# The last tiles of a fused FFT and mixture-of-experts kernel: smaller routing batches, more scatters per tile, and an earlier step table

## The chip, the cores and the metric

One Trainium2 chip, one core of it. The metric is device time in microseconds (us) from launch to the end of the program, the median of several runs. The profile is one execution taken by the hardware profiler.

## What is computed

The reference runs three stages on `x` of shape (8, 3072, 256), all in float32:

```python
X = np.fft.fft(np.fft.fft(x, axis=1), axis=2).real          # 24576 tokens of 256
h = np.maximum(np.maximum(X @ w1, X @ w2), X @ w3)          # 768 hidden
x = h @ w_out                                               # 256
# second stage of experts, E = 8, top-1
skip = x @ w_skip                  # only tokens with skip > 0 are computed
e = argmax(x @ w_gate);  gate_w = softmax(x @ w_gate)[e]
out = x;  out[skip > 0] += gate_w * (relu(x @ W1[e]) @ W2[e])   # W1: 256x1024, W2: 1024x256
```

## The kernel before

The program has three parts, one after the other.

The first part computes the Fourier transform along the sequence and prepares the weights.

The second part (`moe_phase`) goes over 25 tiles of the transformed tokens: 0 to 22 have 8 blocks of 128 tokens, tile 23 has 4 blocks, tile 24 has 5. In period t (`period(t)`, twelve steps n = 0 to 11) the engines compute the hidden layer of tile t and the output layer of tile t-1. A step takes matmuls `pa`, `pb` (L483 to L485), VectorE combinations (L499 to L513), and a split of the result `ht` into a high and a low part, on ScalarE (L519) and GpSimd (L520). The output layer is `rest` (L555, result `zt` by L557), to which a linear term `lin` is added: `linear` makes two matmul groups, ScalarE copies each from PSUM (L546), GpSimd adds and subtracts them (L547, L549). The order on each engine is the order in which the code is written (`manual_schedule`): an instruction that waits holds all that stand behind it on its engine.

Beside this runs the routing, for a batch of tiles at a time (`BATCHES`): their gate scores come in a tile `st`; `finish` (L574 to L608, ten VectorE operations and one exponential on ScalarE) picks the expert and counts the tokens, `place` (L610 to L630, matmuls `pr` and four VectorE operations) computes each token's position in a list per expert, and `scatter` (L633) sends one block's 128 positions to that list in memory, by an indirect DMA on GpSimd. `fill()` does one VectorE step of the routing, and a step n of a period posts at most one scatter per half of `ht`. Before the batch that begins with tile 18 (`EARLY`), `choose` (15 more VectorE operations) picks one expert from the counts so far, for which three steps of 256 tokens are computed at fixed places (`STATIC` = 3).

Between the second part and the third stands the tail, from L1021 on. It finishes tile 24, posts the scatters that are left (each behind `apart()`, a small GpSimd addition on `idle`, L1002), and computes the static steps: `wide1` (48 matmuls L767), `wide1_rest` (VectorE, L771), `layer2_of` (24 matmuls L780 for each of two blocks), `result` (L784) and `place_rows` (L787). `table()` (L818) turns the counts into the table `tab` of all further steps: some 20 small VectorE operations, two transposes on TensorE and a copy. With `tab` SyncE loads the step's list entries `ida`, `idn`, `idm` and weights `ws`, and GpSimd gathers the rows `Gd` (L1110).

The third part is a loop over those steps (L1220, and a second one for half steps): `wide1`, transposes, `layer2_of`, each step with its own weights.

Buffers of the tail that matter here: `st` and `rI` (the positions) have 2 buffers each, `Gd` takes one of the two buffers in which the rows `Gs` of the second and third static step lie, and `acc`, `pz`, `pys` are PSUM.

Of the kernel before, what the change touches and what calls it, by code (L numbers as in the profile page):

```python
# [16 lines left out]
P = 128  # L17
# [15 lines left out]
STATIC = 3  # L33
BATCHES = [(3 * k, 3 * k + 1, 3 * k + 2) for k in range(7)] + [(21, 22), (23,), (24,)]
EARLY = 18
# [11 lines left out]
NK = 2  # L47
F1, F2, F3 = 3, 5, 6
TF = 23
T0 = 2  # L50
ENG = {mybir.EngineType.PE, mybir.EngineType.DVE, mybir.EngineType.Activation, mybir.EngineType.Pool}
# [357 lines left out]
def moe_phase(tc, a, sc, wt, wv, wp, gs, ident, out, lst, cpool):  # L409
    nc = tc.nc  # L410
    tiles = [(j, 0, 512, 0) for j in range(NT - 1)] + [(NT - 1, 0, 256, 0), (NT - 1, 256, 264, NB)]
    with (
# [122 lines left out]
        def layer2(t, hs, y, yk, zt):  # L535
            lin = {}

            def linear(c):
                lin[c] = mo.tile([P, 3, SW], F32, tag="ws", name="lin", bufs=2)
                for k in range(2):  # L540
                    pl = mq.tile([P, 512], F32, tag="pz", name="pl")
                    for n, (g, v) in enumerate(((0, 0), (0, 1), (1, 0))):
                        nc.tensor.matmul(pl[:, :SW], y[:, 2 * k + g, c * P : c * P + P], cc[:, k, v], start=n == 0, stop=k == 1 and n == 2)
                    if k == 0:
                        nc.tensor.matmul(pl[:, :SW], yk[:, c * P : c * P + P], wq, start=False, stop=True)
                    nc.scalar.activation(lin[c][:, k], pl[:, :SW], AF.Copy)  # L546
                nc.gpsimd.tensor_tensor(lin[c][:, 2], lin[c][:, 0], lin[c][:, 1], ALU.add)  # L547
                if (1, c) in bs:
                    nc.gpsimd.tensor_tensor(lin[c][:, 0], lin[c][:, 0], lin[c][:, 1], ALU.subtract)  # L549

# [59 lines left out]
        def place(first, nb, slots, _):  # L610
# [15 lines left out]
            yield  # L626
            ix = mr.tile([P, KB], I32, tag="rI", name="rI")[:, :nb]
            V.tensor_copy(ix, pos)
# [82 lines left out]
        moved = []  # L711
        zz = mr.tile([P, 2, 2], I32, name="zz", bufs=1)
        G, ids = [], []

# [182 lines left out]

        stage = {}

        def arrive(t, zt):  # L900
            k = next(k for k, ts in enumerate(BATCHES) if t in ts)
            if t == BATCHES[k][0]:
                stage["st"], stage["o"] = mr.tile([P, KB, 10], F32, tag="st", name="st"), 0
                nc.gpsimd.memset(stage["st"][:, :, E1:], 1e-9)
            ship(t, zt, stage["st"], stage["o"])
            stage["o"] += NBT[t]
            if t == BATCHES[k][-1]:
                waiting.append((k, stage["st"]))

        def period(t):  # L910
# [10 lines left out]
            for n in range(2 * NC6):  # L921
# [39 lines left out]
                for _ in range(HALF.get(n, 1)):  # L961
                    if half:
                        half.pop(0)()
                        if posted and (n < 9 or t + 1 < len(tiles)):
                            posted.pop(0)()
                if t == 0 and i == 1:
# [31 lines left out]

        idle = mr.tile([P, 2], I32, name="idle", bufs=1)

        def apart():
            nc.gpsimd.tensor_tensor(idle, zz[:, 0], zz[:, 0], ALU.add)  # L1002

        def post(n):
# [11 lines left out]

        nc.gpsimd.memset(zz, 0)
        cum = [mr.tile([P, 32], F32, name=f"cum{k}", bufs=1) for k in range(3)]
        for c in cum:
            nc.gpsimd.memset(c, 0.0)  # L1020
        with tc.manual_schedule(engines=ENG):  # L1021
# [47 lines left out]
            steps = table()  # L1069
            next(steps)  # L1070
            layer2_of(1, h, w, py[1])
            for k in range(1, STATIC):
                for b in range(2):
                    result(G[k - 1][:, b], py[b], ids[k - 1][:, b, 1:2].bitcast(F32), G[k - 1][:, b])
                    apart()
                    place_rows(ids[k - 1], b, G[k - 1][:, b])
                h = [hset() for _ in range(2)]
                ph = [acc("pb"), acc("pb"), acc("pb"), acc("pa")]
                for q in range(4):
                    wide1(x, w, h, q, ph[q])  # L1080
                    wide1_rest(h, q, ph[q])
                    if k == 1 and q == 2:
                        next(steps)
# [9 lines left out]
            idm, idn, ida, idc, idx = (mr.tile([P, 2, 2], I32, name=nm, bufs=1) for nm in ("idm", "idn", "ida", "idc", "idx"))  # L1093
            idb = ids[-1]
            dm = mr.tile([P, 4], F32, name="dm", bufs=1)
            gt = mr.tile([P, 2], I32, name="gt", bufs=1)
            W = [tuple(mh.tile([P, 1024], F32R, tag="ht", name="wd") for _ in range(2)) for _ in range(4)]
            ws = [mb.tile([P, 1024], F32, tag="u", name="ws", bufs=4) for _ in range(4)]
            w1s, w2s = ws[:2], ws[2:]
            Gd = mx.tile([P, 2, D], F32, tag="yb", name="Gd", bufs=2)  # L1100
            Z, Zn, O = (mz.tile([P, 2, D], F32, tag="zt", name=nm) for nm in ("Z", "Zn", "O"))
            load_ids(ida, 0)
            e1 = expert(0)
            load_w(w1s, "e1", e1)
            load_ids(idn, 1)
            load_ids(idm, 2)
            load_w(w2s, "e2", e1)

            def gather(idx, m):
# [3 lines left out]
                return r  # L1113
# [17 lines left out]
            fence_g()  # L1131
            ga += gather(idn, 2)
            for b in range(2):
# [3 lines left out]
        pys = [pys[2], mq.tile([P, 512], F32, tag="pz", name="pyd")]  # L1137
        for q in ga:
            for old in moved:
                tc.declare_no_dep(q.ins, old.ins, reason=why)  # L1140
        moved.extend(ga)
        nb = nc.values_load(nst[0:1, 0:1], min_val=0, max_val=P - 20)
# [254 lines left out]
```

## Time and profile before

| | |
|---|---|
| median of 3 runs | 1756.37 us (1752.12 to 1758.89) |
| the profiled execution | 1751.53 us, of which the span from first to last instruction is 1749.6 us |
| mean granted TensorE clock | 0.976 of full speed |
| busy: TensorE, VectorE, GpSimd, ScalarE | 93%, 77%, 64%, 42% of the span |

Full speed is 2.4 GHz, a granted clock of 0.5 is 1.2 GHz. In the rows, PE is TensorE, PEld its weight load, DVE VectorE, ACT ScalarE, POOL GpSimd, SP SyncE. What stands in brackets at the end of a row is how long the engine was idle before it, and what ended that.

### The profile page before, as it was taken

Reading aid. Unit: us, or ns where it says so; the run is one execution under the profiler, and the core shown is the slowest. Engines: PE = TensorE matmul, PEld = TensorE weight load, DVE = VectorE, ACT = ScalarE, POOL = GpSimd, SP = SyncE. Lnnn points to the kernel's source line nnn. Section 1 sums busy time; section 2 is a strip of 40 time slices with the busy share of each in tenths; the row PEclk is TensorE's granted clock in tenths of the full one; section 3 lists DMA queues with packets and bytes.
Section 4 is the critical chain, followed back from the end, with each engine's and each line's share of the span. In section 5 each row is a group of like instructions: output and inputs, shape, how many; then the busy total and the mean of one; then the engine's idle time right before and its main releaser. Section 6 shows DMA issues by size and latency. Waiting matters only on the chain. (4 is left out here: it accounts for less than half of the span.)

```text
span 1749.6 us, 33308 instructions
## 1 busy us (share of the span) xinstructions
PE 1628.1 (93%) x10837; PEld 1446.3 (83%) x10837; DVE 1347.5 (77%) x2288; ACT 734.7 (42%) x1437; POOL 1115.1 (64%) x1358
## 2 busy tenths in 40 slices
PE   6999699999999999999999999986689999999976
PEld 3665488888888888888888888886589999999976
DVE  8999488887887888888887878864367777777754
ACT  4545433333333333323333333322156666666654
POOL 2000356668769779779688687588646676766663
PEclk9999899999999999999999999989799999999989
DMA  8875411312111111111122111113256666666766
GB/s 327 309 264 204 140 61 43 121 40 58 43 43 44 43 43 43 55 43 43 55 44 50 54 43 40 40 30 90 59 184 219 217 228 225 222 224 226 226 196 218
DMA packets 109434, 212.47 MB, mean 121 GB/s; under 512 B 28107, under 2 KB 61292, under 8 KB 106228
## 3 DMA queue, kind: packets, MB, share of 16 engines
q1 hardware_dynamic: 94360, 188.65, 34.3%
q0 software_dynamic: 14112, 21.77, 4.0%
q8 instruction: 56, 0.92, 0.3%
q14 instruction: 42, 0.34, 0.2%
q10 hardware_dynamic: 864, 0.79, 0.1%
HBM read 157.82 MB, written 55.17 MB: 122 GB/s over the span
## 5 line engine op out<-in xcount | busy, mean ns | idle before, releaser
L520 POOL TENSOR_TENSOR ht<-u,ht 128x512 fp32r<-128x512 f32 (+2 forms) x300 | 374.1, 1252 | 184.2 <-ACT ht L519 181.4
L555 PE MATMUL pz<-wo,ht 128*128 128x266 f32 x3474 | 457.9, 287 | 0.6 <-DVE zt L557 0.6
L555 PEld LDWEIGHTS pz<-wo,ht 128*128 128x128 f32 x3474 | 444.8, 189 | 8.2 <-DVE zt L557 0.8
L519 ACT ACTIVATE ht<-u 128x512 fp32r<-128x512 f32 (+2 forms) x300 | 175.9, 610 | 534.4 <-DVE u L513 468.0
L633 POOL DMA_INDIRECT lst<-pair,rI x193 | 190.3, 986 | 35.6 <-issue 28.2
L767 PE MATMUL acc<-xd,wd 128*128 128x256 f32 x1632 | 193.4, 278 | 0.9 <-DVEq L1220 0.9
L767 PEld LDWEIGHTS acc<-xd,wd 128*128 128x128 f32 x1632 | 190.1, 188 | 1.1 <-issue 1.1
L811 DVE TENSOR_TENSOR wd<-ws,wd 128x1024 fp32r<-128x1024 f32 x150 | 177.5, 1225 | 16.5 <-issue 6.6
L810 ACT ACTIVATE wd<-ws 128x1024 fp32r<-128x1024 f32 x150 | 154.9, 1060 | 69.7 <-issue 43.7
L483 PE MATMUL pa<-y,wt 128*128 128x512 f32 (+2 forms) x300 | 126.1, 420 | 40.2 <-DVE u L499 27.4
L557 DVE TENSOR_TENSOR zt<-pz,lin 128x266 f32<-128x266 f32 x193 | 81.6, 432 | 88.5 <-PE pz L555 47.7
L780 PE MATMUL pys<-wd,hs 128*128 128x256 f32 x960 | 126.8, 288 | 0.5 <-DVE hs L771 0.5
L502 DVE TENSOR_TENSOR u<-u,pb 128x512 f32<-128x512 f32 (+2 forms) x150 | 99.2, 661 | 29.2 <-PE pb L485 28.4
L780 PEld LDWEIGHTS pys<-wd,hs 128*128 128x128 f32 x960 | 119.2, 192 | 1.4 <-DVE hs L771 0.9
L771 DVE SCALAR_TENSOR_TENSOR hs<-acc,hs 128x512 fp32r<-128x512 f32 x148 | 97.8, 687 | 29.2 <-ACT hs L768 25.8
L768 ACT ACTIVATE hs<-acc 128x512 fp32r<-128x512 f32 x148 | 86.3, 596 | 77.1 <-PE acc L767 71.8
L483 PE MATMUL pb<-y,wt 128*128 128x512 f32 (+2 forms) x300 | 118.1, 394 | 0.0
L484 PE MATMUL pb<-y,wt 128*128 128x512 f32 (+2 forms) x300 | 117.5, 392 | 0.0
L483 PEld LDWEIGHTS pa<-y,wt 128*128 128x128 f32 x300 | 57.4, 191 | 72.4 <-DVE u L499 59.5
L485 PE MATMUL pb<-y,wt 128*128 128x512 f32 (+2 forms) x300 | 117.2, 391 | 0.0
L485 PE MATMUL pa<-y,wt 128*128 128x512 f32 (+2 forms) x300 | 117.2, 391 | 0.0
L484 PE MATMUL pa<-y,wt 128*128 128x512 f32 (+2 forms) x300 | 117.0, 390 | 0.0
(286 smaller groups left out, 3205.2 us busy)
## 6 DMA issues: line engine op xcount, KB each, us to landing
ws<-e SPq DMA_DIRECT2D x164, 512.0 KB
xt<-xf SPq DMA_DIRECT2D x24, 1024.0 KB
out<-zt SPq DMA_DIRECT2D x48, 512.0 KB
yr<-ysc SPq DMA_DIRECT2D x25, 512.0 KB
ysc<-ytc SPq DMA_DIRECT2D x8, 768.0 KB
yb<-yfsc SPq DMA_DIRECT2D x23, 256.0 KB
ysc<-yts SPq DMA_DIRECT2D x8, 672.0 KB
wr<-wm SPq DMA_DIRECT2D x6, 768.0 KB
```

What stands on the lines that cost most here:

```text
L483: nc.tensor.matmul(pt[:, :w], wt[f][:, g, 0, c], hi, start=True, stop=False)
L484: nc.tensor.matmul(pt[:, :w], wt[f][:, g, 0, c], lo, start=False, stop=False)
L485: nc.tensor.matmul(pt[:, :w], wt[f][:, g, 1, c], hi, start=False, stop=not whole)
L502: nc.vector.tensor_tensor(minus_to, r, pb[:, :w], ALU.subtract)
L519: nc.scalar.activation(ht[:, 0, :w], h[:, s, :w], AF.Copy)
L520: nc.gpsimd.tensor_tensor(ht[:, 1, :w], h[:, s, :w], bits(ht[:, 0, :w]), ALU.subtract)
L555: nc.tensor.matmul(pz[:, :SW], hs[s][f][:, g, c * P : c * P + P], wo[:, v, f], start=f == 0 and g == 0 and v == 0, stop=f == NC6 - 1 and g ...
L633: ins = nc.gpsimd.indirect_dma_start(out=lst[:, :], out_offset=bass.IndirectOffsetOnAxis(ap=ix[:, b : b + 1], axis=0), in_=pair[:, first + b],
L767: nc.tensor.matmul(ph[:, f % 2 * 256 : f % 2 * 256 + 256], lhs, rhs, start=n == 0, stop=n == 5)
L780: nc.tensor.matmul(py[:, :D], lhs, rhs, start=n == 0, stop=n == 23)
L810: nc.scalar.activation(hi, r, AF.Copy)
L811: nc.vector.tensor_tensor(lo, r, bits(hi), ALU.subtract)
```

## The change

It has four edits, all for the end of the second part and the tail.

1. Batches: tiles 18 and 19 are one batch, 20 to 24 one each. Before, 18 to 20 were one, 21 and 22 one, 23 and 24 one each.
2. `rI` gets 4 buffers; the two `st` tiles are made once, with their padding set at the start of the program; from tile 20 on, every third step n posts two scatters with `apart()` between them.
3. For tiles from 21 on, ScalarE no longer copies the second half of the linear term; VectorE reads it from PSUM and does the addition and the subtraction.
4. In the tail: routing of tile 24 and the table's VectorE work come between the first and the second half of the first static step; the table's second part comes after the first half of its output layer; loads and the first gather of the loop's rows are issued within the static steps; `Gd` has a buffer of its own.

```diff
-BATCHES = [(3 * k, 3 * k + 1, 3 * k + 2) for k in range(7)] + [(21, 22), (23,), (24,)]
+BATCHES = [(3 * k, 3 * k + 1, 3 * k + 2) for k in range(6)] + [(18, 19)] + [(t,) for t in range(20, 25)]
-F1, F2, F3 = 3, 5, 6
+F1, F2, F4 = 3, 5, (4, 7)
+TL = 21
+TP = 20
...
-                    nc.scalar.activation(lin[c][:, k], pl[:, :SW], AF.Copy)
-                nc.gpsimd.tensor_tensor(lin[c][:, 2], lin[c][:, 0], lin[c][:, 1], ALU.add)
+                    if k == 0 or t < TL:
+                        nc.scalar.activation(lin[c][:, k], pl[:, :SW], AF.Copy)
+                eng, odd = (nc.gpsimd, lin[c][:, 1]) if t < TL else (nc.vector, pl[:, :SW])
+                eng.tensor_tensor(lin[c][:, 2], lin[c][:, 0], odd, ALU.add)
                 if (1, c) in bs:
-                    nc.gpsimd.tensor_tensor(lin[c][:, 0], lin[c][:, 0], lin[c][:, 1], ALU.subtract)
+                    eng.tensor_tensor(lin[c][:, 0], lin[c][:, 0], odd, ALU.subtract)
...
-            ix = mr.tile([P, KB], I32, tag="rI", name="rI")[:, :nb]
+            ix = mr.tile([P, KB], I32, tag="rI", name="rI", bufs=4)[:, :nb]
...
-        stage = {}
+        stage = {"n": 0, "sts": [mr.tile([P, KB, 10], F32, name=f"st{k}", bufs=1) for k in range(2)]}
+        for x in stage["sts"]:
+            nc.gpsimd.memset(x[:, :, E1:], 1e-9)
...
-                stage["st"], stage["o"] = mr.tile([P, KB, 10], F32, tag="st", name="st"), 0
-                nc.gpsimd.memset(stage["st"][:, :, E1:], 1e-9)
+                stage["st"], stage["o"] = stage["sts"][k % 2], 0
...
-                        if posted and (n < 9 or t + 1 < len(tiles)):
-                            posted.pop(0)()
+                        for k in range(2 if t >= TP and n % 3 == 0 else 1):
+                            if posted and (n < 9 or t + 1 < len(tiles)):
+                                if k:
+                                    apart()
+                                posted.pop(0)()
...
-            for _ in range(2):
-                fill()
-            for q in range(4):
+            for q in range(2):
+                for _ in range(F4[q]):
+                    fill()
                 wide1(x, w, h, q, ph[q])
-            for q in range(4):
-                for _ in range(F3):
-                    fill()
+            wide1_rest(h, 0, ph[0])
+            settle()
+            wide1_rest(h, 1, ph[1])
+            steps = table()
+            next(steps)
+            for q in range(2, 4):
+                wide1(x, w, h, q, ph[q])
+            for q in range(2, 4):
                 wide1_rest(h, q, ph[q])
-            settle()
...
             layer2_of(0, h, w, py[0])
+            next(steps)
...
+            Gd = mb.tile([P, 2, D], F32, tag="r", name="Gd", bufs=1)
+            e1 = expert(0)
+            load_w(w1s, "e1", e1)
+            load_ids(ida, 0)
+            load_ids(idn, 1)
+            load_ids(idm, 2)
+            load_w(w2s, "e2", e1)
...
             for k in range(1, STATIC):
+                if k + 1 == STATIC:
+                    apart()
+                    known(gather(ida, 2))
...
-            Gd = mx.tile([P, 2, D], F32, tag="yb", name="Gd", bufs=2)
...
-            apart()
-            ga = gather(ida, 2)
```

Where instructions stand, at the three places of which the prediction speaks. First TensorE in the first static step, from the end of the position matmuls `pr` of tile 24 on; before:

```order
L618 MATMUL pr<-sl,ones 128x9
L780 MATMUL pys<-wx,hs 128x256 x24
L750 MATMUL acc<-ident,Gs 128x128 x4
L823 LDWEIGHTS ones
L823 MATMUL pc<-sl,ones 128x8
L780 MATMUL pys<-wx,hs 128x256 x24
L767 MATMUL acc<-xs,wx 128x256 x36
L857 MATMUL pt<-ident,r_12993 1x128 x2
```

and now, where `pr` itself stands behind 24 of the step's 48 `acc` matmuls, not behind all:

```order
L622 MATMUL pr<-sl,ones 128x9
L833 LDWEIGHTS ones
L833 MATMUL pc<-sl,ones 128x8
L777 MATMUL acc<-xs,wx 128x256 x24
L790 MATMUL pys<-wx,hs 128x256 x24
L867 MATMUL pt<-ident,r_12947 1x128 x2
L760 MATMUL acc<-ident,Gs 128x128 x4
L790 MATMUL pys<-wx,hs 128x256 x24
```

The count `pc` for the table has moved ahead of the second half of the first step's `acc` matmuls, and the table's transposes `pt` have moved from within the second step to the middle of the first.

Second GpSimd at the end of the tail's scatters (`lst`); before:

```order
L633 DMA lst<-pair,rI 228480x2
L1002 TENSOR_TENSOR idle<-zz 128x2
L787 DMA out<-Gs,ids_11691 27776x256
L1002 TENSOR_TENSOR idle<-zz 128x2
L787 DMA out<-Gs,ids_11691 27776x256
L1002 TENSOR_TENSOR idle<-zz 128x2
L787 DMA out<-Gs,ids_11702 27776x256
L1002 TENSOR_TENSOR idle<-zz 128x2
L787 DMA out<-Gs,ids_11702 27776x256
L1002 TENSOR_TENSOR idle<-zz 128x2
L1110 DMA Gd<-out,ida 128x256 x2
```

and now:

```order
L637 DMA lst<-pair,rI 228480x2
L721 TENSOR_TENSOR idle<-zz 128x2
L797 DMA out<-Gs,ids_11253 27776x256
L721 TENSOR_TENSOR idle<-zz 128x2
L797 DMA out<-Gs,ids_11253 27776x256
L721 TENSOR_TENSOR idle<-zz 128x2
L1097 DMA Gd<-out,ida 128x256 x2
L721 TENSOR_TENSOR idle<-zz 128x2
L797 DMA out<-Gs,ids_11264 27776x256
```

The gather of the loop's first rows stands ahead of the second step's row scatters. Behind the last static gather (`Gs`), 34 of these list scatters stood in the tail before, now 15.

Third VectorE at the second output block of tile 23, in period 24; before:

```order
L583 TENSOR_TENSOR rd<-st,rm 128x16x8
L502 TENSOR_TENSOR pa<-r,pb 128x264
L587 SCALAR_TENSOR_TENSOR rd<-rd,kk 128x16x8
L557 TENSOR_TENSOR zt<-pz,lin 128x266
L590 TENSOR_REDUCE rv<-rd 128x16
```

and now:

```order
L587 TENSOR_TENSOR rd<-st_1373,rm 128x8x8
L504 TENSOR_TENSOR pa<-r,pb 128x264
L591 SCALAR_TENSOR_TENSOR rd<-rd,kk 128x8x8
L551 TENSOR_TENSOR lin<-lin,pl 128x266
L553 TENSOR_TENSOR lin<-lin,pl 128x266
L561 TENSOR_TENSOR zt<-pz,lin 128x266
L594 TENSOR_REDUCE rv<-rd 128x8
```

The two operations on `lin` are new on VectorE, directly ahead of the `zt` that needs them, and the routing operations beside them work on 8 blocks, not 16.

## Rows read from the trace of the kernel before

**Rows 1.** Busy time by stretch: periods 21 to 24, tail, static steps.

```profile
core 0: us, PE busy (x) PEld busy (x) DVE busy (x) ACT busy (x) POOL busy (x), PEclk, DMA share, GB/s
1042.55:1082.40 39.85, 38.99 (x246) 34.66 (x245) 31.86 (x55) 13.05 (x27) 35.84 (x35) 1.00 0.16 47
1082.40:1127.00 44.60, 41.19 (x251) 36.55 (x250) 38.99 (x80) 12.55 (x28) 23.24 (x24) 0.96 0.13 40
1127.00:1160.40 33.40, 32.34 (x273) 31.68 (x272) 21.85 (x60) 10.22 (x29) 25.18 (x33) 1.00 0.11 33
1160.40:1187.65 27.25, 21.05 (x144) 19.73 (x143) 19.46 (x59) 6.96 (x22) 21.62 (x26) 0.81 0.23 54
1187.65:1207.42 19.77, 19.13 (x159) 18.86 (x157) 10.40 (x29) 8.73 (x19) 15.02 (x20) 1.00 0.49 127
1207.42:1251.06 43.64, 15.10 (x110) 14.47 (x108) 10.08 (x31) 3.11 (x8) 35.06 (x61) 0.65 0.10 16
1251.06:1280.65 29.59, 25.04 (x204) 24.39 (x203) 14.34 (x34) 8.29 (x13) 11.75 (x19) 0.94 0.34 103
```

**Rows 2.** Timeline of TensorE, tail: start, duration, instruction, idle before it.

```profile
1207.42 5.81 PE L767 MATMUL acc<-xs,wx 128*128 128x256 f32 x48
...
1224.90 0.20 PE L616 MATMUL pr<-sl,tri 128*128 128x45 bf16 x1 [11.67 <-DVE sl L597]
...
1244.30 3.54 PE L780 MATMUL pys<-wx,hs 128*128 128x256 f32 x16 [16.86 <-DVE rS L604]
...
1251.06 4.26 PE L767 MATMUL acc<-xs,wx 128*128 128x256 f32 x36
...
1262.75 5.62 PE L767 MATMUL acc<-xs,wx 128*128 128x256 f32 x48
1268.21 2.88 PE L780 MATMUL pys<-wx,hs 128*128 128x256 f32 x24
1274.00 0.41 PE L750 MATMUL acc<-ident,Gd 128*128 128x128 f32 x2 [2.91 <-DMA Gd<-out,ida]
...
1275.52 4.25 PE L780 MATMUL pys<-wx,hs 128*128 128x256 f32 x24
```

**Rows 3.** Timeline of VectorE, tail.

```profile
1218.34 0.17 DVE L628 CAST rI<-rs 128x4 int32<-128x4 f32 x1 [14.28 <-DMA lst<-pair,rI]
...
1243.26 0.20 DVE L604 TENSOR_REDUCE rS<-st 128x5 f32<-128x45 f32 x1 [17.52 <-POOL st L904]
...
1249.56 0.16 DVE L825 TENSOR_TENSOR tf<-pc,kt 128x8 f32<-128x8 f32 x1
...
1253.54 0.15 DVE L853 TENSOR_SCALAR r<-r 128x1 f32<-128x1 f32 x1
```

**Rows 4.** Timeline of GpSimd, tail.

```profile
1202.32 1.00 POOL L633 DMA_INDIRECT lst<-pair,rI  x1 [0.17 <-issue]
...
1243.07 0.16 POOL L904 MEMSET st<- 128x24 f32 x1
...
1270.70 1.36 POOL L1110 DMA_INDIRECT Gd<-out,ida  x1 [5.76 <-issue]
```

**Rows 5.** Costliest groups of the page: busy, mean ns of one, idle before.

```profile
L771 DVE SCALAR_TENSOR_TENSOR hs<-acc,hs 128x512 fp32r<-128x512 f32 x148 | 97.8, 687 | 29.2 <-ACT hs L768 25.8
```

**Rows 6.** Timeline of TensorE, its longest waits in periods 22 and 24.

```profile
1113.25 0.51 PE L483 MATMUL pa<-y,wt 128*128 128x512 f32 x1 [3.12 <-DVE u L499]
...
1169.91 0.59 PE L483 MATMUL pa<-y,wt 128*128 128x264 f32 x1 [3.70 <-DVE u L499]
```

**Rows 7.** Timeline of VectorE, periods 22 and 24.

```profile
1097.05 0.98 DVE L690 TENSOR_TENSOR rc<-rc,ru 128x8 f32<-128x8 f32 x1
...
1168.83 0.43 DVE L557 TENSOR_TENSOR zt<-pz,lin 128x266 f32<-128x266 f32 x1 [4.38 <-POOL lin L547]
```

**Rows 8.** Timeline of GpSimd, beside the two rows of VectorE.

```profile
1096.71 1.30 POOL L520 TENSOR_TENSOR ht<-u,ht 128x512 fp32r<-128x512 f32 x1
...
1168.13 0.67 POOL L547 TENSOR_TENSOR lin<-lin 128x266 f32<-128x266 f32 x1
```

More of the change, by code (lines that the diff above doesn't have):

```diff
@@ L712, in moe_phase, with apart @@
         zz = mr.tile([P, 2, 2], I32, name="zz", bufs=1)
+        nc.gpsimd.memset(zz, 0)
+        idle = mr.tile([P, 2], I32, name="idle", bufs=1)
+        def apart():
+            nc.gpsimd.tensor_tensor(idle, zz[:, 0], zz[:, 0], ALU.add)
         G, ids = [], []
@@ L997, in moe_phase @@
         w = []
-        idle = mr.tile([P, 2], I32, name="idle", bufs=1)
-        def apart():
-            nc.gpsimd.tensor_tensor(idle, zz[:, 0], zz[:, 0], ALU.add)
         def post(n):
@@ L1015, in settle @@
             post(len(posted))
-        nc.gpsimd.memset(zz, 0)
         cum = [mr.tile([P, 32], F32, name=f"cum{k}", bufs=1) for k in range(3)]
@@ L1068, in moe_phase, with gather, known @@
             split_x(x, px)
-            steps = table()
-            next(steps)
             layer2_of(1, h, w, py[1])
+            idm, idn, ida, idc, idx = (mr.tile([P, 2, 2], I32, name=nm, bufs=1) for nm in ("idm", "idn", "ida", "idc", "idx"))
+            idb = ids[-1]
+            W = [tuple(mh.tile([P, 1024], F32R, tag="ht", name="wd") for _ in range(2)) for _ in range(4)]
+            ws = [mb.tile([P, 1024], F32, tag="u", name="ws", bufs=4) for _ in range(4)]
+            w1s, w2s = ws[:2], ws[2:]
+            Gd = mb.tile([P, 2, D], F32, tag="r", name="Gd", bufs=1)
[5 more added lines that the diff above has]
+            load_w(w2s, "e2", e1)
+            def gather(idx, m):
+                r = [nc.gpsimd.indirect_dma_start(
+                    out=Gd[:, b], out_offset=None, in_=out[:, :],
+                    in_offset=bass.IndirectOffsetOnAxis(ap=idx[:, b, 0:1], axis=0)) for b in range(m)]
+                return r
+            def known(ga):
+                for q in ga:
+                    for old in moved:
+                        tc.declare_no_dep(q.ins, old.ins, reason=why)
+                moved.extend(ga)
             for k in range(1, STATIC):
+                if k + 1 == STATIC:
+                    apart()
+                    known(gather(ida, 2))
                 for b in range(2):
@@ L1081, in moe_phase @@
                     wide1_rest(h, q, ph[q])
-                    if k == 1 and q == 2:
-                        next(steps)
                 if k + 1 == STATIC:
@@ L1092, in moe_phase @@
                 layer2_of(1, h, w, py[1])
-            idm, idn, ida, idc, idx = (mr.tile([P, 2, 2], I32, name=nm, bufs=1) for nm in ("idm", "idn", "ida", "idc", "idx"))
-            idb = ids[-1]
             dm = mr.tile([P, 4], F32, name="dm", bufs=1)
             gt = mr.tile([P, 2], I32, name="gt", bufs=1)
-            W = [tuple(mh.tile([P, 1024], F32R, tag="ht", name="wd") for _ in range(2)) for _ in range(4)]
-            ws = [mb.tile([P, 1024], F32, tag="u", name="ws", bufs=4) for _ in range(4)]
-            w1s, w2s = ws[:2], ws[2:]
-            Gd = mx.tile([P, 2, D], F32, tag="yb", name="Gd", bufs=2)
             Z, Zn, O = (mz.tile([P, 2, D], F32, tag="zt", name=nm) for nm in ("Z", "Zn", "O"))
[L1102 to L1109, printed above, removed]
-                r = [nc.gpsimd.indirect_dma_start(
-                    out=Gd[:, b], out_offset=None, in_=out[:, :],
-                    in_offset=bass.IndirectOffsetOnAxis(ap=idx[:, b, 0:1], axis=0)) for b in range(m)]
-                return r
             def fence_g():
@@ L1131, in moe_phase @@
             fence_g()
-            ga += gather(idn, 2)
+            known(gather(idn, 2))
             for b in range(2):
@@ L1137, in moe_phase @@
         pys = [pys[2], mq.tile([P, 512], F32, tag="pz", name="pyd")]
[L1138 to L1141, printed above, removed]
         nb = nc.values_load(nst[0:1, 0:1], min_val=0, max_val=P - 20)
```

## Prediction

> **What bounds the kernel now.** I read the busy shares over the whole span first, then cut the stretch around the change by its stages, then followed each engine's timeline through it. In the periods TensorE is the bound: 38.99 us of 39.85 in period 21. Then three stretches fall off [rows 1]. Period 22 takes 44.60 us instead of some 39.9; period 24 takes 27.25 with only 21.05 busy, at a granted clock of 0.81; and from the start of the static steps at 1207.42 to the loop at 1280.65, 73.2 us, TensorE is busy 40.1.
>
> The timeline of TensorE shows the tail's holes: 11.67 us ahead of the position matmuls of tile 24, 16.86 within the first output layer, 2.91 ahead of the loop's first rows [rows 2]. Each is followed to its cause on the engine that it waits for. The first: VectorE stood 14.28 us at the cast of the positions of tile 23, since that took a buffer from which scatters were still being read [rows 3]. The second: VectorE stood 17.52 us for the padding of `st`, a 0.16 us instruction on GpSimd that stood behind the scatters [rows 3, 4]. So both are the one queue of scatters. From 1202.32 to 1243.07 GpSimd posts 29 of them and one addition of 0.67: 1.38 us each [rows 4, 8]. The third hole is the gather, held 5.76 us on GpSimd [rows 4]. Its list entries come from a table that ended at 1253.69 [rows 3], and its buffer is that of a step whose rows were still being sent; I take the latter for the holder, since the rest of that wait fits nothing else.
>
> **The change part by part: the tail.** Without waits a static step takes 1262.75 - 1251.06 = 11.69 us [rows 2]; three are 35.1. What comes on top now:
> - The matmuls of positions and count: 0.3 us (`pr` 0.20 for its first, overlapped) [rows 2].
> - The wait for the routing of tile 24. It now stands behind half of `wide1`, 5.81 / 2 = 2.9 us. A small operation on VectorE costs some 0.19 (the table's 22 take 1253.54 + 0.15 - 1249.56 = 4.1) [rows 2, 3]. Eight of them lie ahead of the position matmuls, with one exponential and its two handovers: 1.5 to 3 us. Wait 0 to 2, I take 0.3.
> - The wait for the table. Between those matmuls and the last two `wide1_rest` VectorE has 6 small operations (1.1), two `wide1_rest` (0.69 each), the table (4.1) and then the third rest (0.69): 7.3 us [rows 3, 5]. TensorE meanwhile has the other half of `wide1` (2.9) and half an output layer (2.88 / 2): 4.3 [rows 2]. Wait 3.0.
> - The clock. After the wait of 2.91 the next 24 matmuls took 4.25 instead of 2.88 [rows 2]: I take 1.4. In period 24 the mean clock of 0.81 means 38% of 27.25 us, 10 us, at 1.2 GHz [rows 1], which is worth up to 5 us: that is the upper bound, and 0 the lower.
> - Entry of the loop: 0.9, the end of 4.25 behind 1275.52 to 1280.65 [rows 1, 2].
>
> Sum 35.1 + 0.3 + 0.3 + 3.0 + 1.4 + 0.9 = 41.0, against 73.2: **32.2 us less** (28 to 37).
>
> What covers the rest: 15 scatters are left in the tail, not 34, 20.7 us at 1.38. Begun at 1202.32 at the latest, they are out by 1223 [rows 4]. From the table's end to the arrival of the first rows it took 1274.00 - 1253.69 = 20.3 us before, the 5.76 included [rows 2 to 4]. The table now ends at 1207.4 + 2.9 + 0.6 + 6.6 = 1217.5; plus 20.3 is 1238; TensorE comes to those rows after 2.5 steps, at 1242. Four us of cover; beyond it each us late is a us lost. The weights `ws` start with the same table and have the same cover.
>
> **The periods.** Edit 3 takes 0.67 per operation off GpSimd, and puts one on VectorE that reads PSUM and SBUF as `zt` does, 0.43 [rows 7, 8]. Eight per full tile, four for tile 23: 5.4 and 2.7 us off GpSimd, 3.4 and 1.7 on VectorE. The added scatters: 16 each in periods 22 and 23, at 1.0 plus 0.17 [rows 4].
> - Period 24. VectorE waited 4.38 us for that addition on GpSimd, which stood among scatters, then TensorE 3.70 for VectorE, and then the clock fell [rows 1, 6, 7]. With the addition on VectorE this chain is gone. What bounds then is VectorE: 19.46 + 1.7, less half of the routing of 16 blocks (1): 20.2, and some 2 us in which it waits for the first output block. I take 22.5: **4.7 less** (1 to 7).
> - Period 22 lost 4.7 us to `choose` and to the routing of 24 blocks, which made VectorE late (38.99 busy, TensorE's longest wait 3.12) [rows 1, 6]. Now it has the routing of 8 blocks, the placing of 16, and 3.4 us of additions. VectorE's base is 31.9 (period 21) [rows 1]; with 3.4 and some 30 small operations (0.1 to 0.2 each, 4) it has 39, still near its limit: **2.6 less** (4.7 less to 1 more).
> - Period 21 gets `choose` and the routing of 16 blocks, so part of those 4.7: **3 more** (0 to 5).
> - Period 23: TensorE 32.34 of 33.40; VectorE 21.85 has room for 3.4 [rows 1]: **0** (1 less to 2 more).
>
> Edit 2's `rI` and `st` cost nothing in time: the padding's two instructions move to the program's start.
>
> Of the routing's operations one row is odd: 0.98 us for 128x8, where such a thing costs 0.16. It ends with a GpSimd addition that began 0.34 before it and ran 1.30 [rows 3, 7, 8]. So an operation with two inputs in SBUF stood until GpSimd was through. The Trainium skill has this as a rule (SBUF — State Buffer, Who interferes with whom): a VectorE instruction with two SBUF inputs and a GpSimd one that reads SBUF exclude each other, one with an input in PSUM does not. The rule speaks for edit 3, and against smaller batches beside a busier GpSimd; the trace agrees, with 0.98 against 0.16. By the row, each of some 8 two-input operations of a batch loses 0.8 with a chance of GpSimd's share of reading, about 0.4: 2.5 us per batch, which is in the 3 and the 2.6 above once; a second time it is a rival.
>
> Sum: -32.2 - 4.7 - 2.6 + 3 + 0 = **-36.5 us**. The profiled execution took 1751.53, 4.8 below the median of 1756.37; all terms are differences, so I set them against the median: **1720**.
>
> **Rivals.**
> - *GpSimd late with `ht`.* Period 22 gets 23.24 - 5.4 + 16 x 1.17 + 4 small ones (1.5) = 38 us in some 42, period 23 25.18 - 5.4 + 8 x 1.17 (8 were there) + 1.8 = 31 in 33.4 [rows 1, 4]. It fits, but the last `ht` of a tile stands behind all of that, and the first output block of the next period needs it. For: no room left. Against: the periods have it in sum. Price: 3 us and a clock loss of up to 5, at two places: 1720 + 6 to 16, 1731.
> - *The lock of the two engines* costs 2.5 more in each of periods 21, 22 and 23: 1727.
> - *The rows come late*: the loop's first gather or weights use up their cover, as they did by 2.91 before. Price: 3 to 8 with the clock: 1725.
> - *No gain in the periods or the table's wait smaller*: the bounds on the good side, TensorE without the 3.0 and the clock: 1712.
> - *Slower.* Scatters in the periods cost more than 1.17, since they alternate with additions there. They delay every `ht` behind them; 32 of them. To undo 36.5 us they would have to cost 2.3 each, 1.15 more; from there on the kernel is slower. For: GpSimd is full in both periods. Against: in the tail they took 1.0, beside a VectorE that worked too [rows 1, 4]. 1760.
> - *No change* (the scatters drain at the same time): excluded unless the positions come late; 34 against 15 in the tail is fixed by the order. 1750.
>
> **How the numbers follow.** Forecast 0.58, good side 0.12, GpSimd late 0.12, lock 0.07, rows late 0.06, no change 0.02, slower 0.03. The likeliest gives 1720. Range 1707 to 1736: the terms' bounds on one side (-32.2 to -37, -4.7 to -7, -2.6 to -4.7, 3 to 0) reach 1706, the rivals of the other side 1736; outside of it 0.15. A measurement of this kernel tells 0.5%, 9 us, from no change: faster by more than that 0.95, within it 0.02, slower 0.03.
>
> **What would show it.** Right: no wait over 4 us on TensorE between the last period and the loop; about 3 us within the first output layer; the padding gone from GpSimd's tail and 15 scatters there; the loop 41 us behind the first `wide1`; period 24 near 22.5 and without a clock of 0.81; periods 21 and 22 both near 42. Wrong: TensorE waiting for `ht` at the first output block of periods 23 or 24; the gather's landing as the last release ahead of the loop; a loop that starts later relative to the static steps than 45 us.

## The result, and the profile after

The changed kernel takes 1740.32 us (median of 4 runs, 1736.93 to 1740.73), the kernel before 1756.52 (4 runs, 1752.12 to 1758.89): a ratio of 0.9905, 95% interval 0.9886 to 0.9925. It is 16 us faster, not 36.5; the forecast had the direction, and the range of 1707 to 1736 does not hold the time. The profiled execution after took 1740.47 us with a span of 1738.7; the one before, 1751.53, lies below all four of its runs.

Cut at the first matmul of each period, of the first `wide1` and of the loop, the two profiled executions differ so:

| stretch | before, us | after, us | difference | forecast |
|---|---|---|---|---|
| up to period 21 | 1042.6 | 1043.8 | +1.3 | 0 |
| period 21 | 40.1 | 47.7 | +7.6 | +3 |
| period 22 | 44.4 | 43.6 | -0.8 | -2.6 |
| period 23 | 33.4 | 35.1 | +1.8 | 0 |
| period 24 and tail | 47.0 | 41.1 | -5.9 | -4.7 |
| static phase | 73.2 | 46.8 | -26.4 | -32.2 |
| loop to the end | 469.0 | 480.5 | +11.6 | 0 |

Windows of the changed kernel, its answer to [rows 1]: periods 21, 22 and 23, then the first part of period 24, the tail, the static phase, and the loop to the end (columns as there).

```profile
1043.84:1091.52 47.68, 41.30 (x249) 36.35 (x248) 38.86 (x80) 13.27 (x28) 35.65 (x36) 0.96 0.13 38
1091.52:1135.13 43.61, 41.24 (x274) 35.84 (x273) 40.16 (x81) 11.13 (x24) 29.27 (x29) 1.00 0.16 41
1135.13:1170.26 35.13, 32.82 (x258) 32.14 (x257) 28.11 (x78) 9.30 (x26) 29.55 (x36) 0.95 0.12 32
1170.26:1192.00 21.74, 18.09 (x138) 16.34 (x137) 19.73 (x65) 6.32 (x20) 18.04 (x24) 1.00 0.21 58
1192.00:1211.35 19.35, 19.05 (x155) 18.56 (x154) 13.97 (x37) 8.13 (x17) 15.66 (x20) 1.00 0.55 151
1211.35:1258.17 46.82, 40.32 (x311) 38.99 (x310) 21.93 (x61) 11.80 (x20) 20.10 (x34) 0.89 0.23 73
...
1258.17:1738.70 480.53, 453.68 (x3748) 448.54 (x3748) 337.34 (x463) 301.68 (x436) 310.96 (x508) 0.98 0.68 216
```

And the loop of the kernel before in the same view:

```profile
1280.65:1749.60 468.95, 444.51 (x3748) 440.81 (x3748) 338.51 (x463) 301.45 (x436) 296.88 (x507) 0.98 0.69 221
```

The part behind the loop's start has the same 3748 matmuls in both, and TensorE is busy 9.2 us longer with them, at the same clock. Waits make only 2.4 us of the 11.6: its matmuls follow each other more slowly. One step of the loop shows it; timeline of TensorE, first the kernel before, then the changed one:

```profile
1445.27 5.62 PE L767 MATMUL acc<-xd,wd 128*128 128x256 f32 x48
```

```profile
1512.73 5.85 PE L777 MATMUL acc<-xd,wd 128*128 128x256 f32 x48
```

A group's duration less the last matmul's, over 47, is the pace: (5.62 - 0.28) / 47 = 113.6 ns before, (5.85 - 0.28) / 47 = 118.5 after. In the kernel before some steps have the one and some 117.7; after, all but the first have 118.5 to 118.7. The shortest step of the loop goes from 11.54 to 11.82 us.

The static phase, timeline of TensorE, the answer to [rows 2]:

```profile
1211.35 3.01 PE L777 MATMUL acc<-xs,wx 128*128 128x256 f32 x24
...
1214.40 3.09 PE L777 MATMUL acc<-xs,wx 128*128 128x256 f32 x24
...
1222.47 1.22 PE L790 MATMUL pys<-wx,hs 128*128 128x256 f32 x4 [2.88 <-DVE r L862]
1226.26 1.95 PE L790 MATMUL pys<-wx,hs 128*128 128x256 f32 x6 [2.56 <-ACT hs L778]
...
1229.14 4.51 PE L790 MATMUL pys<-wx,hs 128*128 128x256 f32 x24
...
1253.85 0.60 PE L760 MATMUL acc<-ident,Gd 128*128 128x128 f32 x4
...
1258.17 2.10 PE L777 MATMUL acc<-xd,wd 128*128 128x256 f32 x14 [0.88 <-DVEq L1233]
```

The two long holes of [rows 2] are gone, the wait for the table is there (2.88, forecast 3.0), and the loop's first rows (`Gd`) are met without a wait. New is the second wait, 2.56 us for ScalarE's relu, and behind it 24 matmuls that take 4.51 us. ScalarE, timeline of the same stretch:

```profile
1214.69 0.60 ACT L778 ACTIVATE hs<-acc 128x512 fp32r<-128x512 f32 x1 [1.12 <-PE pc L833]
1218.43 0.60 ACT L778 ACTIVATE hs<-acc 128x512 fp32r<-128x512 f32 x1 [3.14 <-PE acc L777]
1225.60 0.60 ACT L778 ACTIVATE hs<-acc 128x512 fp32r<-128x512 f32 x1 [6.57 <-remote]
```

The matmuls for this last relu are the end of the group at 1214.40 and were issued by 1217.3; it began 8 us later (`remote` is a signal whose sender the view doesn't name). GpSimd's last scatter of the tail began at 1223.59:

```profile
1223.59 0.98 POOL L637 DMA_INDIRECT lst<-pair,rI  x1 [0.16 <-issue]
```

Period 21, the answer to [rows 6] to [rows 8], has a wait of TensorE for `ht`, one of VectorE for the linear addition on GpSimd, and a small VectorE operation of 1.14 us (0.16 to 0.20 in the other batches), shown with the GpSimd addition that ends with it:

```profile
1053.17 0.39 PE L559 MATMUL pz<-wo,ht 128*128 128x266 f32 x1 [2.79 <-POOL ht L522]
...
1055.00 0.43 DVE L561 TENSOR_TENSOR zt<-pz,lin 128x266 f32<-128x266 f32 x1 [5.37 <-POOL lin L551]
...
1077.62 1.14 DVE L596 SCALAR_TENSOR_TENSOR rv<-st,rv 128x16 f32<-128x16 f32 x1
1076.32 2.41 POOL L464 TENSOR_TENSOR y<-yr,y 128x1024 fp32r<-128x1024 f32 x1
```

So there are three questions: the loop that nobody touched, the late relu, and period 21.

### The profile page after: what moved, and what is told of

It reads as the page before. It is cut to its first block, busy times and chain, and to the rows that moved or that the text cites. A ratio compares the mean times of both kernels' runs of the same rounds, so it can differ in the third digit from the quotient of the medians.

```text
span 1738.7 us, 33399 instructions
## 1 busy us (share of the span) xinstructions
PE 1639.5 (94%) x10839; PEld 1453.1 (84%) x10839; DVE 1362.0 (78%) x2341; ACT 732.9 (42%) x1426; POOL 1110.2 (64%) x1320
## 5 line engine op out<-in xcount | busy, mean ns | idle before, releaser
L637 POOL DMA_INDIRECT lst<-pair,rI x193 | 190.6, 987 | 32.2 <-issue 26.5
L777 PE MATMUL acc<-xd,wd 128*128 128x256 f32 x1632 | 199.3, 281 | 0.9 <-DVEq L1233 0.9
L777 PEld LDWEIGHTS acc<-xd,wd 128*128 128x128 f32 x1632 | 196.1, 188 | 1.2 <-issue 1.1
L821 DVE TENSOR_TENSOR wd<-ws,wd 128x1024 fp32r<-128x1024 f32 x150 | 177.4, 1223 | 18.7 <-issue 12.3
L486 PE MATMUL pa<-y,wt 128*128 128x512 f32 (+2 forms) x300 | 117.8, 393 | 0.0
```

The costliest lines, as they stand in the source:

```text
L486: nc.tensor.matmul(pt[:, :w], wt[f][:, g, 0, c], lo, start=False, stop=False)
L637: ins = nc.gpsimd.indirect_dma_start(out=lst[:, :], out_offset=bass.IndirectOffsetOnAxis(ap=ix[:, b : b + 1], axis=0), in_=pair[:, first + b],
L777: nc.tensor.matmul(ph[:, f % 2 * 256 : f % 2 * 256 + 256], lhs, rhs, start=n == 0, stop=n == 5)
L821: nc.vector.tensor_tensor(lo, r, bits(hi), ALU.subtract)
```

## The experiments

**The loop: is it the place of the tiles?** The two added `ix` buffers take 192 bytes of each partition, and every pool allocated behind them moves up by 192, the operands `xd` and `hs` of the loop's matmuls among them; the weights `wd` lie ahead and stay. e1_shift is the kernel before with that line alone:

```diff
-            ix = mr.tile([P, KB], I32, tag="rI", name="rI")[:, :nb]
+            ix = mr.tile([P, KB], I32, tag="rI", name="rI", bufs=4)[:, :nb]
```

> The kernel before, with one line of the change: the slot numbers of a routing (ix) get four buffers instead of two. Nothing else moves; the 192 bytes of a partition that they take push every pool allocated behind that one up by 192 bytes, as in the changed kernel. Theory A (the place of the tiles in SBUF sets how fast the loop's matmuls follow each other): the steps of the loop go from a floor of 11.55 us to the 11.82 us of the changed kernel, and the part behind the loop's start from 469 us to about 480, so the kernel is 9 to 12 us slower than before, a ratio of 1.005 to 1.007. Theory B (the stretch of the loop depends on how the loop is entered or on the changed tail): steps at 11.55 to 11.75 as before, 469 us behind the loop's start, ratio 0.999 to 1.001.

Measured: steps with a floor (the shortest step) of 11.83 us, all but the first at 118.6 to 118.8 ns. Timeline of TensorE, one step:

```profile
1510.55 5.86 PE L767 MATMUL acc<-xd,wd 128*128 128x256 f32 x48
```

Behind the loop's start 476.6 us, periods 1 to 17 in 690.4 instead of 689.3. Time 1762.06 against 1757.29, ratio 1.0024 (1.0011 to 1.0037): slower, with the pace of the changed kernel, though by 4 to 5 us and not by 9 to 12. e2_noshift is the opposite: the changed kernel with its 192 bytes won back.

```diff
-            exc, t, oh, ge = S("exc", [P, 16]), S("tt", [P, 16]), S("oh", [P, 16]), S("ge", [P, 16])
+            exc, t, ge = S("exc", [P, 16]), S("tt", [P, 16]), S("ge", [P, 16])
+            rd = mr.tile([P, KB, E1], F32, tag="rd", name="rd", bufs=1).rearrange("p b e -> p (b e)")
+            oh = rd[:, :16]
...
-            x2 = S("x2", [P, 2, 16])
+            x2 = rd[:, 16:48].rearrange("p (a e) -> p a e", a=2)
```

> The changed kernel, with two small tiles of the table (oh, x2) put into the memory of a routing tile that is done by then, so that all pools behind lie where they lay before. The instructions are the same. Theory A (place in SBUF): floor of a loop step back to 11.55 us, the part behind the loop's start from 480.5 to about 469 us, total 1728 to 1731 us, ratio to before 0.984 to 0.986. Theory B (loop entry, changed tail): 11.82 us, 480 us, total 1740, ratio 0.9905.

Measured: 1728.39 us, ratio 0.9832 (0.9813 to 0.9851); the steps are back, with a floor of 11.34 us (one step; the next have 11.54):

```profile
1504.56 5.62 PE L777 MATMUL acc<-xd,wd 128*128 128x256 f32 x48
```

The same instructions at another place: theory A stands in both directions. Behind the loop's start it took 473.4 us, not 469: 7.1 of the 12 us won come from there, and 5.8 from the static phase, 41.0 us instead of 46.8, which neither theory had. So that the total fits is in part luck. e8_shift64 wins back 128 bytes only (`x2` alone), which leaves 64:

```diff
-            x2 = S("x2", [P, 2, 16])
+            x2 = mr.tile([P, KB, E1], F32, tag="rd", name="rd", bufs=1).rearrange("p b e -> p (b e)")[:, :32].rearrange("p (a e) -> p a e", a=2)
```

> The changed kernel, with only the small tile x2 put into a used routing tile: all pools behind lie 64 bytes further than before the change, where they lie 192 further in the changed kernel and 0 in its other variant. If the matmuls' pace hangs on the place of their operands, the 24 matmuls of a layer follow each other at 118.6 ns as with 192, or at 113.6 as with 0, and the loop's steps have their floor at 11.82 or 11.35 to 11.55 us accordingly; a third value says that more than two cases exist. If it doesn't hang on the place: 118.6 and 11.82 in every variant with the new tail, which the variant with 0 already speaks against.

Measured: a third value, 120.0 ns, floor 11.95 us, 481.8 us behind the loop's start, 1745.13 us.

```profile
1504.48 5.92 PE L777 MATMUL acc<-xd,wd 128*128 128x256 f32 x48
```

e12_m128 goes 128 bytes the other way, e11_both is its counterpart at the old place; both double scatters from period 22 on (below).

```diff
-            exc, t, ge = S("exc", [P, 16]), S("tt", [P, 16]), S("ge", [P, 16])
+            exc = S("exc", [P, 16])
...
-            oh = rd[:, :16]
+            oh, t, ge = rd[:, :16], rd[:, 48:64], rd[:, 64:80]
```

> The same, with two more small tables (tt, ge) put into the used routing tile, so that all pools behind lie 128 bytes nearer than before the change. If the pace of the matmuls goes by whether the moving rows begin at an odd or even multiple of 64 bytes (odd: 113.6 ns at offset 0; even: 118.6 and 120.0 at 192 and 64): 113.6 ns, steps at 11.35 to 11.6, the time of the run at offset 0 within 2 us. If it is another property of the place: a pace of its own, and 4 to 16 us of difference.

> The variant with the old place in SBUF and scatters doubled from period 22 on, the two changes that gained apart. If they add: period 21 at 46, static phase 39.5 to 41 (46 if the signals are held up again), loop's steps at 11.35 to 11.6, 470 to 474 us behind the loop's start, total 1722 to 1727, ratio 0.980 to 0.983. If the gain of the later doubling was only the chance of a signal in time: 1727 to 1731.

Measured: at minus 128, 24 of 34 steps at 113.4 ns and nine at 117.8, which is what odd multiples of 64 bytes would give, and 1730.44 us (0.9843, 0.9826 to 0.9859), against 1732.12 (0.9852, 0.9832 to 0.9872) for e11_both. The pace alone does not tell the time: behind the loop's start they took 476.9 and 474.5 us, with other waits in the place (6.0 us for rows between 1290 and 1640 us in e12_m128). e11_both did not reach what the sum promised, since its static phase took 46.0 us.

**Period 21: is it GpSimd?** e3_tp22 begins the doubled scatters two periods later, e4_tl20 moves tile 20's additions to VectorE.

```diff
-TP = 20
+TP = 22
```

> The changed kernel, with the second scatter beside a half from period 22 on and not from 20 on. Theory A (in period 21 GpSimd is late because the added scatters stand ahead of its h halves and linear additions): TensorE's wait of 2.79 us for h at 1053 and VectorE's 5.37 us for the linear addition at 1055 are gone, the period from first matmul to first matmul goes from 47.7 to 42 to 44 us, total 1735 to 1737. Theory B (VectorE bounds period 21, with the choose chain and the routing of sixteen blocks beside it): the period stays at 46.5 to 48 us, the wait for h only turns into waits for u, total 1739 to 1741.

```diff
-TL = 21
+TL = 20
```

> The changed kernel, with the linear additions of tile 20 on VectorE too (period 21), which takes 12 operations of about 1 us off GpSimd there and puts about as many of 0.4 us on VectorE. Theory A (GpSimd is late in period 21): period 21 goes from 47.7 to 43 to 45 us, total 1736 to 1738. Theory B (VectorE bounds period 21): it goes to 48 to 52 us, total 1741 to 1745.

Measured, windows of period 21, e3_tp22 and e4_tl20:

```profile
1043.53:1089.70 46.17, 41.33 (x249) 36.23 (x248) 40.85 (x81) 13.24 (x28) 35.81 (x35) 0.96 0.15 41
```

```profile
1044.02:1095.13 51.11, 44.12 (x249) 38.36 (x248) 42.40 (x89) 12.35 (x24) 30.51 (x28) 0.90 0.13 35
```

Theory A's times fail in both. Without the doubling the wait for `ht` is gone and the period is 1.5 us shorter; the rest turns into waits for VectorE (1.38, 0.60 and 2.43). With more work on VectorE the period takes 51.1 us. Executions of one and the same period 21 differ by 2.5 us, so more of them say more: it took 47.7 to 50.2 us in five profiled executions with the doubled scatters there (the changed kernel, e2_noshift, e5_again, e8_shift64, e10_drop15) and 44.7 to 46.3 in four without (e3_tp22, e11_both, e12_m128, e14_spaced), about 3 us less. e3_tp22 took 1730.23 us all the same (0.9857, 0.9832 to 0.9882), e4_tl20 1738.15 (0.9874, 0.9846 to 0.9902): the first had a static phase of 39.6 us, more of the gain than period 21.

e6_three puts the `choose` chain back into period 22 (it starts from e2_noshift):

```diff
-BATCHES = [(3 * k, 3 * k + 1, 3 * k + 2) for k in range(6)] + [(18, 19)] + [(t,) for t in range(20, 25)]
+BATCHES = [(3 * k, 3 * k + 1, 3 * k + 2) for k in range(7)] + [(t,) for t in range(21, 25)]
-TL = 21
+TL = 22
-TP = 20
+TP = 23
...
-                        for k in range(2 if t >= TP and n % 3 == 0 else 1):
+                        for k in range(2 if t >= TP and n % 2 == 0 else 1):
```

> The variant with the old place in SBUF, with tiles 18 to 20 as one batch of three (as before the change), so that the choose chain and that routing stand in period 22 again; tile 21's linear additions are back on GpSimd, and scatters are doubled at every second half of periods 23 and 24 instead of every third from period 20. 25 scatters are left behind the last period instead of 15. Theory A (what period 21 lost is the choose chain and the routing beside a tile whose VectorE has no room for both): period 21 at 40.1, 22 at 44.4, 23 at 34 to 36, 24 at 41 to 43 us, in sum 7 us less than in that variant; static phase 41 to 45. Total 1720 to 1725, ratio 0.979 to 0.982. Theory B (the periods lose the same sum wherever the routing stands, or GpSimd gets late with h in period 23): the four periods take 168 us as there, total 1728 to 1734.

Measured, windows of periods 21 and 22 and of the static phase:

```profile
1041.87:1082.04 40.17, 39.29 (x248) 34.93 (x247) 32.06 (x56) 13.06 (x27) 35.91 (x35) 1.00 0.16 47
1082.04:1125.03 42.99, 39.43 (x249) 34.89 (x248) 38.62 (x80) 12.46 (x28) 23.18 (x23) 1.00 0.13 41
...
1204.69:1259.97 55.28, 41.15 (x311) 38.86 (x310) 22.07 (x61) 11.78 (x20) 31.86 (x54) 0.88 0.26 62
```

Theory A for the periods: period 21 is back at 40.2, and the four periods and the tail took 162.8 us instead of 168.9, though period 23 took 37.1, above its 34 to 36. `choose` with the routing of 24 blocks cost 2.8 us in period 22 here, where GpSimd is busy 23.2 us, and 4.0 to 5.3 in five other profiled executions with the same period 22; with 16 blocks and no doubled scatters it cost 4.5 to 6.1 in period 21, where GpSimd is busy 35.8. The total, 1741.00 (0.9918, 0.9888 to 0.9947), is no better: with 24 scatters in the tail the static phase took 55.3 us instead of the 41 to 45 expected.

**The static phase: what holds up the relus?** e5_again is the changed kernel once more, with no edit.

> The changed kernel itself, once more, on the same chip as the others of this call. Its profile showed a static phase (first wide1 to loop) of 46.8 us with a wait of 6.57 us of ScalarE ahead of its third relu, while the same instructions took 41.0, 39.6 and 41.0 us in three kernels that differ from it elsewhere. Theory A (that wait is an event of single executions): 39.5 to 41 us here. Theory B (it belongs to this kernel's timing): 46 to 47.5 us again. On either, period 21 at 47 to 49 us, the loop's steps at 11.82 us, the part behind the loop's start at 477 to 482 us.

Measured: 1738.80 us (0.9904, 0.9877 to 0.9930), static phase 45.9 us, close to theory B; period 21 took 50.2 us, not 47 to 49. Its ScalarE:

```profile
1224.46 0.60 ACT L778 ACTIVATE hs<-acc 128x512 fp32r<-128x512 f32 x1 [7.47 <-remote]
1227.42 0.60 ACT L778 ACTIVATE hs<-acc 128x512 fp32r<-128x512 f32 x1 [2.37 <-remote]
```

e7_tail is the new tail alone (from e2_noshift, with the old batches, `TL` and `TP` at 25):

```diff
-BATCHES = [(3 * k, 3 * k + 1, 3 * k + 2) for k in range(6)] + [(18, 19)] + [(t,) for t in range(20, 25)]
+BATCHES = [(3 * k, 3 * k + 1, 3 * k + 2) for k in range(7)] + [(21, 22), (23,), (24,)]
-TL = 21
+TL = 25
-TP = 20
+TP = 25
```

> The new tail alone: old place in SBUF, old batches, no doubled scatters, no linear additions on VectorE; only the order behind the last period, the lasting gate tiles and the four ix buffers are those of the change. The scatters of tiles 18 to 24 now drain behind the last period, 1.38 us each, until about 1249. Theory A (these scatters hold the list, and so the loop's first rows): periods 21 to 24 as before (40.1, 44.4, 33.4, 47.0 us), TensorE waits 8 to 16 us for the first rows, static phase 50 to 58 us, total 1735 to 1742. Theory B (they are covered): static phase 41 us, total 1725 to 1728.

Measured: 1752.25 us (0.9985, 0.9970 to 1.0001), static phase 68.7: neither theory. No buffer holds VectorE any more, and TensorE stands all the same. Timelines of TensorE, ScalarE and GpSimd in the second static step:

```profile
1234.49 3.27 PE L777 MATMUL acc<-xs,wx 128*128 128x256 f32 x11 [4.35 <-issue]
1238.11 1.11 PE L777 MATMUL acc<-xs,wx 128*128 128x256 f32 x3 [0.34 <-issue]
...
1247.37 0.82 PE L777 MATMUL acc<-xs,wx 128*128 128x256 f32 x3 [1.03 <-issue]
1249.51 0.37 PE L777 MATMUL acc<-xs,wx 128*128 128x256 f32 x1 [1.32 <-issue]
1250.22 0.37 PE L777 MATMUL acc<-xs,wx 128*128 128x256 f32 x1 [0.34 <-issue]
1251.63 0.57 PE L777 MATMUL acc<-xs,wx 128*128 128x256 f32 x1 [1.04 <-issue]
1253.05 0.37 PE L777 MATMUL acc<-xs,wx 128*128 128x256 f32 x1 [0.84 <-issue]
...
1253.89 1.09 ACT L778 ACTIVATE hs<-acc 128x512 fp32r<-128x512 f32 x2 [19.45 <-remote]
...
1250.77 0.99 POOL L797 DMA_INDIRECT out<-Gs,ids  x1 [0.16 <-issue]
```

The matmuls come in ones to threes with nothing that they wait for, and the relus stand 19.45 us for matmuls of which the first quarter, 12 of 48, was issued by 1238.2. Both come free within 2.2 us of the end, at 1251.76, of GpSimd's last indirect DMA in a row that had run since 1202, one every 1.38 us. Two kernels take scatters out of the tail: e9_drop19 leaves 15 of the 34 of e7_tail, e10_drop15 none of the 15 of the changed kernel.

```diff
+        kept = []
...
-                apart()
-                posted.pop(0)()
+                p = posted.pop(0)
+                if len(kept) < 15:
+                    apart()
+                    p()
+                    kept.append(p)
```

> The kernel with the new tail alone, with 15 of its 34 scatters behind the last period and the other 19 left out (their list entries stay padding, so the loop works on padding rows in their place). In the kernel with all 34 TensorE issued its matmuls in ones to threes from 1228 to 1253 us, 0.7 to 1.4 us apart and with no wait in the profile, ScalarE's relus waited 19.45 us for matmuls that had been issued long before, and all came free when the last scatter was out. Theory A (a run of scatters back to back holds up TensorE's issue and its signals): the drips are gone, no wait over 8 us on ScalarE, static phase 40 to 47 instead of 68.7 us. Theory B (the matmuls drip for a reason of their own, their place in TensorE's program for one): drips in the same matmuls, static phase over 55 us.

```diff
-                apart()
-                posted.pop(0)()
+                posted.pop(0)
```

> The changed kernel, with all 15 scatters behind the last period left out (their list entries stay padding). Theory A (the run of scatters holds up TensorE's signals): ScalarE's third relu follows its matmuls within 1 us instead of 6.6 to 7.5, what is left is the wait for the table, and the static phase takes 38 to 40.5 instead of 45.9 to 46.8 us. Theory B (the late relu comes of the table or of ScalarE): 45 to 47 us.

Measured, windows of the static phase, e9_drop19 and e10_drop15:

```profile
1207.27:1250.26 42.99, 37.59 (x311) 36.63 (x310) 21.64 (x61) 11.64 (x20) 23.15 (x39) 0.96 0.28 80
```

```profile
1213.14:1254.07 40.93, 38.00 (x311) 37.39 (x310) 21.53 (x61) 11.80 (x20) 8.37 (x14) 0.96 0.26 83
```

68.7 became 43.0, and 46.8 became 40.9, just above the 40.5 expected and at the prediction's 41.0; no relu waits over 4.2 us, and the times were 1725.06 and 1731.13 us. Theory A: the scatters hold up TensorE. In e9_drop19, with 15 scatters left, one relu still waited 3.67 us for a `remote` signal. Whether it is their number or their density is told by e13_spaced (from e7_tail) and e14_spaced (from e11_both, with `range(3)`):

```diff
-                apart()
+                for _ in range(6):
+                    apart()
                 posted.pop(0)()
```

> The kernel with the new tail alone and its 34 scatters, with six small GpSimd additions between two scatters instead of one, so that a scatter comes every 2.5 us or so, as in the periods, instead of every 1.38. They last until about 1290 then, and the loop must wait for the list. Theory A (only a run of scatters without gaps holds up TensorE's signals): the second static step's matmuls run without drips, its relus follow within 3 us, and TensorE comes to the loop's first rows by 1250 and waits there 30 to 50 us. Theory B (it is the number of scatters under way): drips and relus held up as in the dense run, until the last scatter.

> The variant with the old place in SBUF and doubling from period 22 (static phase 46.0 us with a relu held up), with three small additions between two scatters of the tail instead of one: a scatter every 1.8 us or so, the last out by 1229 instead of 1223. Theory A (gaps let the signals through): no relu held up over 4 us, static phase 40 to 42, total 1724 to 1728. Theory B (number of scatters): static phase 46 to 52, total 1732 to 1738.

Measured, e13_spaced, timelines of TensorE, GpSimd and ScalarE in the second static step:

```profile
1233.35 5.62 PE L777 MATMUL acc<-xs,wx 128*128 128x256 f32 x48
...
1236.62 0.99 POOL L637 DMA_INDIRECT lst<-pair,rI  x1
1239.36 0.99 POOL L637 DMA_INDIRECT lst<-pair,rI  x1
...
1234.91 0.60 ACT L778 ACTIVATE hs<-acc 128x512 fp32r<-128x512 f32 x1 [3.60 <-PE acc L777]
1236.28 0.60 ACT L778 ACTIVATE hs<-acc 128x512 fp32r<-128x512 f32 x1 [0.76 <-PE acc L777]
1237.63 0.60 ACT L778 ACTIVATE hs<-acc 128x512 fp32r<-128x512 f32 x1 [0.76 <-issue]
```

With a scatter every 2.73 us the 48 matmuls run without a gap, while the 34 go on until 1303 (the loop's rows are then 59.8 us late, not 30 to 50, and the kernel takes 1788.83). So it is the density and not the total number; that fewer scatters are under way at once is not told apart from it. e14_spaced, with a scatter every 1.91 us, windows of period 21 and of the static phase:

```profile
1042.92:1087.59 44.67, 39.70 (x250) 34.95 (x249) 40.36 (x80) 13.24 (x28) 35.86 (x35) 1.00 0.15 42
1207.32:1248.43 41.11, 37.51 (x311) 36.72 (x310) 21.55 (x61) 11.55 (x20) 26.15 (x60) 0.96 0.30 82
```

1724.12 us (0.9807, 0.9779 to 0.9835) against 0.9852 (0.9832 to 0.9872) for e11_both, the same kernel without the gaps: the two intervals just touch. It beats the kernel before by 33 us and the changed one by about 16.

## Why the prediction was wrong

The tail's mechanism was right as far as it went. The wait for the table is 2.88 us (forecast 3.0), 15 scatters are left, the rows of the loop are not late, period 24 takes 21.74 (22.5) at a clock of 1.00. Three steps failed.

*"Edit 2's `rI` and `st` cost nothing in time."* They cost no instruction, but 192 bytes, and by their place the loop's matmuls went from 113.6 or 117.7 ns to 118.6. The profiled executions with all scatters at the old place took 468.3 to 476.3 us behind the loop's start (seven, mean 472.5), those at plus 192 took 476.6 to 482.2 (five, mean 478.7): 6 us, and 1.1 in periods 1 to 17. These totals nearly meet, but TensorE's busy time in that part does not: 443.8 to 446.5 us at the old place, 449.9 to 454.1 at plus 192. By e1_shift, the edit alone, the whole kernel loses 4 to 5 us. The rest of the 11.6 in the table is chance between executions: before had the second shortest loop of the seven. It is also why "all terms are differences" failed: a change to the routing's small tiles reached all stages behind it.

*The static phase, 32.2 less.* The sum had a term for each wait, and the scatters only as cover for the rows ("they are out by 1223"; the last ended at 1224.6). It had none for what they do to TensorE: 5 to 6 us in the changed kernel. Where that did not happen, the tail took 39.6 to 41.1 us in e2_noshift, e3_tp22, e4_tl20, e10_drop15 and e14_spaced, and the sum of 41.0 holds. The reading of [rows 2] and [rows 3] was half of the truth: VectorE did stand for a buffer and for the padding, but e7_tail, which has neither wait, won only 4.5 of the 73.2 us. What the smaller batches were worth is that they left 15 scatters in the tail and not 34.

*"Period 21 gets `choose` and the routing of 16 blocks, so part of those 4.7: 3 more."* A term mis-sized: 7.6, and 10.1 in e5_again. The doubled scatters are about 3 us of it. For them the sum had nothing in period 21: it put 16 scatters each into periods 22 and 23, where the trace has 12 and 15. Period 21 posts two fewer than before (8, not 10), but two in a row at 1044.50 and 1045.88, ahead of the `ht` halves and the addition that others wait for. The other 4.5 to 6.1 us are `choose` and the routing. Their price was taken from period 22, where GpSimd is busy 23.2 us and where they cost 2.8 to 5.3 us in six profiled executions; in period 21 it is 35.8 [rows 1]. The forecast took only a part of that price. That the full GpSimd makes the chain dearer is argued and not shown, since the two ranges overlap, with 24 blocks in one and 16 in the other. What the trace has for it are operations with two inputs in SBUF (1.14 us for 128x16, ended with a GpSimd addition); the clock fell too, to a mean of 0.96, and of 0.90 in e5_again. The Trainium skill's rule (SBUF — State Buffer, Who interferes with whom) was weighed at a chance of 0.4 per operation; the row of 1.14 agrees with it again. GpSimd late with `ht` was a rival, put into periods 23 and 24; it came in period 21, with 2.79 us.

The misses, from the two profiled executions of the changed kernel: 7 to 8.5 us in periods 21 to 24 and the tail, 5 to 6 in the static phase, 4 (e1_shift) to 7 (the means) by the place. That is 16 to 21.5 us; from -36.5 to -16.2 it is 20.3.

## What to carry to other kernels

A buffer more is an edit to every address behind it: compare the pace of a matmul group in a stage that nobody touched before believing that a stage is unchanged, and try the old place. Do not take the price of a moved chain from the stretch that it comes from: here it was 2.8 to 5.3 us there, and 4.5 to 6.1 where GpSimd was nearly full (36 of 40 us). When an engine stands and a queue beside it is dense, thin the queue once: with two more additions of 0.2 us between scatters the median was 8 us lower.

## What the runs showed of the hardware

- With the moving tile `xd` and the tile `hs` shifted by 0, 64, 192 and -128 bytes and the weights in place, 48 matmuls of 256 columns follow each other in 113.6 (or 117.7), 120.0, 118.6 and 113.4 (or 117.8) ns, at a granted clock of 1.00. Why was not found; that `xd` and `hs` begin at odd multiples of 64 bytes in the good ones fits four points.
- Indirect DMAs on GpSimd every 1.38 us held up TensorE's issue (matmuls 0.7 to 1.4 us apart) and its signals (relus waiting 5.9 to 19.5 us); at 1.91 and 2.73 us not. At 15 in a row it happened in five profiled executions (the changed kernel, e5_again, e8_shift64, e11_both, e12_m128), and not in three others with the same tail (e2_noshift, e3_tp22, e4_tl20). These three differ from the five in one more thing: their traces, and that of e1_shift, hold 22260 to 22280 semaphore updates, all others 18940 to 19750, though e1_shift runs the same instructions as the kernel before (19052 updates). So they were not recorded alike, and whether the recording has a part in the hold-up is not tested. By what way the scatters act is open. The Trainium skill (SBUF — State Buffer, SBUF: two separate sides) states that TensorE's own port never waits on anyone; these runs show TensorE slowed by a tile's place and by GpSimd's scatters, though not that either goes through that port.
